# Second unit's queries and values fetched behind six weight items, and the first unit's last scores ahead of dummy products

## The chip, the cores and the metric

The kernel runs on one core of a Trainium2 chip. The metric is the device time of one execution in microseconds (us), the median of several runs. Before the change it is 558.18 us (three runs: 558.14, 558.18 and 559.48).

A core has five instruction queues, each in order: PE (matrix products; PEld are its weight loads), DVE (vector engine), ACT (scalar engine, with lookup functions), POOL (a second, slower vector engine) and SP (issues most transfers). ACT issues a few transfers too. The transfers of SP's queue and of ACT's queue are carried by the same 16 DMA engines.

## The reference

An attention-like recurrence over 768 tokens for 4 batches of 8 heads of width 48, followed by a two-layer network of width 2048 with an ELU. Cut to what matters:

```python
f = 1.0 / (1.0 + np.exp(-f_logit))
for t in range(S):
    state = f[:, :, t, :, None] * state + np.einsum('bhd,bhe->bhde', k[:, :, t], v[:, :, t])
    y[:, :, t] = np.einsum('bhd,bhde->bhe', q[:, :, t], state)
x = y.transpose(0, 2, 1, 3).reshape(B * S, H * D)          # 3072 tokens x 384
h = x @ w_in                                               # 384 -> 2048
g = np.where(h > 0.0, h, np.exp(np.minimum(h, 0.0)) - 1.0)
out = g @ w_out                                            # 2048 -> 384
```

The weights reach the chip as 8-byte floats and are turned into 4-byte floats there.

## The kernel before

The 3072 tokens are cut into 12 **units** of 256 tokens. A unit's attention is computed in a chunked form (four chunks of 64 tokens), its result `xt` is 384 x 256, and the network then runs over it in eight pieces of 256 of the 2048 inner columns. All of it is one list per engine, written out by hand in program order (`manual_schedule`); a dictionary `plan` attaches attention work of unit u+1 and weight work to numbered steps T of the network, two steps to a piece: `up(P)` at even T (h = x @ w_in for a piece), `down(P - 2)` at odd T. From unit 1 on the products use seven instead of eight blocks (`up7`), for which POOL prepares differences of blocks of `xt` (`blend`, line 892) and of weights (`mix`, line 885).

**Attention of a unit.** The 8 heads lie as four pairs; the fourth pair (number `NKT` = 3) has its gates spread over gap rows of the other three and gets them by a transfer from SBUF to SBUF (`move`, line 643, two transfers each). `gates` (lines 617 and 619) makes 1 + exp(-f) on ACT; `grow` (631) is a running product on DVE; `fall` (636) its reciprocal; `scale` (626) multiplies k by the one and q by the other on POOL. `transposed` (674) turns k by products with the identity, `advance` (737) makes the state updates of the chunks, `scores` (714) the products of k and q, `mask` (722) zeroes the later tokens on DVE, `step` (695, 700) carries the state from chunk to chunk. For unit 0 `first_outputs` (817) makes the result from scores, values and states, and ACT and DVE copy it to `xt0` (827, 829), after which the network starts (`up(0)`, line 949). For unit 1 `both(1)` at step 8 runs `advance`, `scores`, `mask` and `step`; its transposes are at step 2, its `move(1, 1)` is issued by ACT at step 3, `carried(1)` ends its result at step 11 and sends the fourth pair's rows to the gap rows of `xt1` by two transfers from ACT (line 784). `blend(1)` waits for these, and `up(8)`, the first piece of unit 1 (line 904), for `blend(1)`.

**Weights.** There are 16 items of 768 KB, in the order in which they are needed: w_in pieces 0, 1, 2, then w_out 0, w_in 3, w_out 1, w_in 4 (items 0 to 6), w_out 2 (item 7), w_in 5 (item 8), w_out 3 (item 9), w_in 6, w_out 4, w_in 7, w_out 5, 6, 7 (items 10 to 15). `fetch(n)` issues one from SP: a w_out item is one transfer (line 549), a w_in item is one large (551) and two small ones for the gap rows (554). There are seven landing buffers (`area`, `AHEAD` = 7), so `fetch(n + 7)` stands behind `merge(n)`. An item is converted by `split` (568 and 572, DVE), `lower` (578, ACT) and `merge` (586, DVE). The first two items (`HOLD` = 2) are fetched at once; items 2 to 6 wait for a small POOL memset of their buffers (line 1142) that POOL reaches behind its work for unit 0.

**Dummy products.** `warm(n)` (line 1074) issues n products of the identity of 128 x 512 whose results nobody uses.

**What orders the transfers.** Each transfer reports to one of eight completion semaphores, handed out in turn over SP's and ACT's transfers together, and its issue waits until the transfer before it on the same semaphore has landed. SP issues in order, so one waiting issue holds all behind it.

Of the kernel before, what the change touches and what calls it, by code (L numbers as in the profile page):

```python
# [356 lines left out]
def fast(ctx: ExitStack, tc: tile.TileContext, q, k, v, f_logit, w_in, w_out, out, flag, outer):  # L357
# [18 lines left out]
    nc = tc.nc  # L376
# [10 lines left out]
    HP = H // 2  # L387
    NFT = DFF // 128
    NKT = DM // 128
# [36 lines left out]
    qkf = [  # L426
        {n: cst.tile([128, HP, 2, U] if n == "f" else [128, HP, U], FP32, name=f"{n}{i}") for n in "fqk"}
        for i in range(NB)
    ]
# [5 lines left out]
    def load(u, names="fkqv"):  # L435
        b, s0 = u // UPB, (u % UPB) * U
        for n in names.replace("v", ""):
            to = qkf[u % NB][n][MAIN]
            frm = src[n][b, :, :, s0 : s0 + U].rearrange("(p r) d s -> (r d) p s", r=2)
            if n == "f":  # L440
                to, frm = to[:, 0:NKT, 0], frm[:, 0:NKT]
            nc.sync.dma_start(out=to, in_=frm)
            for r in range(2 if n == "f" or n == "k" and u > 1 else 0):
                gap = qkf[u % NB][n][GAP[r] : GAP[r] + PAD, 0:NKT]
                nc.sync.dma_start(
                    out=gap[:, :, 0] if n == "f" else gap,
                    in_=src[n][b, 2 * NKT + r, :, s0 : s0 + U].rearrange("(i j) s -> i j s", i=PAD),
                )
        if "v" in names:
            nc.sync.dma_start(  # L450
                out=vs[u % NB][:, :, PAD : PAD + DM], in_=v[b, s0 : s0 + U].rearrange("(c t) n -> t c n", t=W)
            )
# [86 lines left out]
    def fetch(n):  # L539
        if n >= NFT:  # L540
            return
        j, out_ = parts[n]
        c = slice(j * 256, (j + 1) * 256)
        to = wo[:, 2 * j : 2 * j + 2] if out_ else wi[j][:]
        if wide:
            raws[n] = area[:, n % AHEAD]
            to = raws[n].rearrange("p (k f) -> p k f", k=to.shape[1])
        if out_:
            nc.sync.dma_start(out=to, in_=w_out[c, :].rearrange("(n p) f -> p n f", n=2))
            return  # L550
        nc.sync.dma_start(out=to[MAIN], in_=w_in[0 : NKT * 2 * D, c].rearrange("(k q) f -> q k f", k=NKT))
        rest = w_in[NKT * 2 * D :, c].rearrange("(r d k) f -> r d k f", r=2, d=PAD)
        for r in range(2):
            nc.sync.dma_start(out=to[GAP[r] : GAP[r] + PAD], in_=rest[r])
# [19 lines left out]
    def lower(n):  # L574

        if wide and n < NFT:
            raw = raws[n]
            nc.scalar.activation(raw.bitcast(U16)[:, 2::4], raw.bitcast(U32)[:, 0::2], AF.Copy, scale=2.0**-29)  # L578

    def merge(n):  # L580
        if wide and n < NFT:
            hi = raws.pop(n).bitcast(I32)[:, 1::2]
            j, out_ = parts[n]
            to = wo[:, 2 * j : 2 * j + 2] if out_ else wi[j][:]
            bits, hi = (x.rearrange("p (k f) -> p k f", k=to.shape[1]) for x in (held.pop(n)[:], hi))
            nc.vector.tensor_tensor(out=to.bitcast(I32), in0=bits, in1=hi, op=ALU.add)
        fetch(n + AHEAD)
# [24 lines left out]
    def gates(u, pieces=(NKT,), bias=1):  # L612

        p = 0
        for n in pieces:
            a = qkf[u % NB]["f"][:, p : p + n, 0]
            nc.scalar.activation(a, a, AF.Exp, scale=-1.0)
            if bias:
                nc.scalar.activation(a, a, AF.Copy, bias=1.0)
            p += n  # L620

    def scale(u, *todo):

        t = qkf[u % NB]
        for n, p, e in todo:
            e.tensor_tensor(out=t[n][:, p], in0=t[n][:, p], in1=t["f"][:, p, "kq".index(n)], op=ALU.mult)  # L626

    def grow(u, p):

        g = qkf[u % NB]["f"][:, p, 0]  # L630
        nc.vector.tensor_tensor_scan(out=g, data0=g, data1=g, initial=1.0, op0=ALU.mult, op1=ALU.max)

    def fall(u, p):

        f = qkf[u % NB]["f"]
        nc.vector.reciprocal(f[:, p, 1], f[:, p, 0])  # L636

    def move(u, which, queue):

        f = qkf[u % NB]["f"]  # L640
        for r in range(2):
            to = PAD + D * r
            queue.dma_start(out=f[to : to + D, NKT, which], in_=f[GAP[r] : GAP[r] + PAD, 0:NKT, which])
# [10 lines left out]
    def watch(u):  # L654
        nc.vector.scalar_tensor_tensor(
            out=fine[:], in0=qkf[u % NB]["f"][:, 0:NKT, 0, U - 1 :], scalar=LIMIT, in1=fine[:],
            op0=ALU.is_le, op1=ALU.mult,
        )
# [44 lines left out]
    def scores(u, banks=("a0", "a1"), pairs=range(HP), pc=None):  # L703

        t = qkf[u % NB]
        if pc is None:
            ats[u] = sb.tile([128, 2, NW, HP, C], FP32, tag="at", name=f"at{u}", bufs=1)
            pc = [ps.tile([128, NW, HP, C], FP32, tag=banks[r], name=f"psS{u}_{r}") for r in range(2)]
        for p in pairs:
            for w in range(NW):  # L710
                for b in range(2):
                    cols = slice(w * W + b * C, w * W + b * C + C)
                    for r in range(2):
                        nc.tensor.matmul(  # L714
                            pc[r][FULL[b], w, p], lhsT=t["k"][FULL[r], p, cols], rhs=t["q"][FULL[r], p, cols],
                            start=True, stop=True,
                        )
        return pc
# [8 lines left out]
    def advance(u, pairs=range(HP)):  # L727

        if u not in pus:
            pus[u] = [ps.tile([128, NW, HP, D], FP32, tag=n, name=f"psU{u}_{n}") for n in ("a0", "a1")]  # L730
        pu = pus[u]
        for p in pairs:
            for w in range(NW):
                for r in range(2):
                    h = 2 * p + r
                    for b in range(2):
                        nc.tensor.matmul(  # L737
                            pu[b][FULL[r], w, p], lhsT=kn[FULL[b], p, w, FULL[r]],
                            rhs=vs[u % NB][FULL[b], w, PAD + h * D : PAD + (h + 1) * D],
                            start=(w == 0 and p == 0), stop=(w == NW - 1 and p == HP - 1), skip_group_check=True,  # L740
                        )
# [91 lines left out]
    def at_step(step, *todo):  # L833
        plan.setdefault(step, []).extend(todo)
# [233 lines left out]
    def warm(n, bank="m0", small=0):  # L1068

        pw = ps.tile([128, 4, 128], FP32, tag=bank, name="psW")  # L1070
        for _ in range(small):
            nc.tensor.matmul(pw[0:1, 0, 0:1], lhsT=ident[:, 0:1], rhs=ident[:, 0:1], start=True, stop=True)
        for _ in range(n):
            nc.tensor.matmul(
                pw[:], lhsT=ident[:], rhs=ident[:].unsqueeze(1).broadcast_to([128, 4, 128]), start=True, stop=True
            )
# [1 line left out]

    gates(0, (1, 2))
    fetch(0)  # L1080
    load(1, "kqv")
    for n in range(1, HOLD):
        fetch(n)
    warm(W0, "m3")
# [7 lines left out]
    fall(0, 0)  # L1092
    scale(0, ("q", 0, nc.gpsimd))
    warm(WA, "m3")
    gates(1, bias=0)
    advance(0, (0, 1))
    pc = scores(0, ("m2", "m3"), (0,))
    nc.gpsimd.tensor_copy(
        even_v[:, :, :, PAD:],
        vs[0][:, :, PAD : PAD + NKT * 2 * D].rearrange("t w (p r d) -> t w p r d", r=2, d=D)[:, :, :, 0],  # L1100
    )
    fall(0, 1)
    scale(0, ("k", NKT, nc.gpsimd), ("q", 1, nc.gpsimd))
    fall(0, 2)
    move(0, 1, nc.scalar)
    warm(4)
    transposed(0, 1, "m1", (1,))
    advance(0, (2,))
    scores(0, None, (1,), pc)
    scale(0, ("q", 2, nc.gpsimd))  # L1110
    advance(0, (3,))
    scores(0, None, (2,), pc)
    nc.gpsimd.tensor_copy(
        padded_v[:, :, :, PAD : 2 * PAD].rearrange("t w (r j) k -> t w r j k", r=2),
        vs[0][:, :, PAD + NKT * 2 * D : PAD + DM].rearrange("t w (r k j) -> t w r j k", r=2, j=NKT),
    )
    a = qkf[1]["f"][:, 0:NKT, 0]
    nc.vector.tensor_scalar_add(a, a, 1.0)
    for p in range(NKT):
        grow(1, p)  # L1120
    move(1, 0, nc.sync)
    scale(0, ("q", NKT, nc.gpsimd))
    warm(2)
    scores(0, None, (NKT,), pc)
    warm(1)
    fall(1, 0)
    split(0)
    for c in range(NC - 1):
# [13 lines left out]
        nc.gpsimd.memset(area[:, HOLD:].bitcast(I32)[:, :, 0:1], 0)  # L1142
    for n in range(HOLD, AHEAD):
        fetch(n)
    merge(0)
    first_outputs(0)
    first_outputs(1)
    lower(1)
    scale(1, ("k", 0, nc.gpsimd), ("q", 0, nc.gpsimd), ("k", 1, nc.gpsimd), ("k", 2, nc.gpsimd))
    scale(1, ("k", NKT, nc.gpsimd))  # L1150
    fall(1, 2)
    watch(0)
    watch(1)
    scale(1, ("q", 1, nc.gpsimd), ("q", 2, nc.gpsimd))
    at_step(A1[2], lambda: outputs(1, ("m3", "m0")), lambda: lower(A1[2]), lambda: lower(A1[2] + 1))
    for n in range(1, NFT):
        t = min(max(needs[n][0] - 2, 0), n) + 2 * (n == NFT - 1)
# [105 lines left out]
```

## Time and profile before

| | us |
|---|---|
| runs, median (lowest, highest) | 558.18 (558.14, 559.48) |
| profiled execution: its own time | 559.46 |
| profiled execution: span of the trace | 557.7 |
| PE busy in the span | 543.0 (97%) |
| DVE / ACT / POOL busy | 406.4 / 228.3 / 287.8 |
| PE busy in 0 to 14, 14 to 28, 28 to 42, 42 to 56, 56 to 70, 70 to 84 | 10.12, 11.47, 11.96, 13.79, 13.24, 14.00 |

The profile is one execution, taken by the hardware profiler; its own time is 1.76 us more than the span of the trace, and lies at the upper of the times seen. The timeline lists instructions by start (us from the start of the span), duration, engine, source line, operation, output and inputs, with the idle time of the engine before them in brackets and what ended it. Stretches give the busy time of each engine in a window, the clock granted to PE as a share of full speed, the mean busy share of the DMA engines, and GB/s. The list of waits gives for an engine and line the total wait in us, how often, and the longest. A product of 4-byte floats stands as two matrix instructions, so `warm(2)` shows as x4.

### The profile page before, as it was taken

To read this page: it belongs to the slowest core of one execution; us is meant where nothing else is said; L and a number is where in the kernel's file an instruction comes from. 1 tells how busy PE (TensorE), PEld (TensorE's weight loads), DVE (VectorE), ACT (ScalarE), POOL (GpSimd) and SP (SyncE) were. 2 spreads that over 40 slices of the span, in tenths; PEclk is the share of its full clock that TensorE was granted. 3 is DMA by queue.
4 is the path that set the end of the run, shared out by engine and by line. 5 is a ranking of instruction groups with operands and counts; after the bars stand their busy time and mean duration, and the time that the engine had idled before them with its cause. 6 is when DMAs were issued, how large, how long until landed. Compare 5 with 4: busy or idle time off the path is not lost.

```text
span 557.7 us, 15617 instructions
## 1 busy us (share of the span) xinstructions
PE 543.0 (97%) x6358; PEld 507.9 (91%) x6358; DVE 406.4 (73%) x804; ACT 228.3 (41%) x443; POOL 287.8 (52%) x559
## 2 busy tenths in 40 slices
PE   7889999999999999999999999999999999999996
PEld 3477679999999999999999999999999999999996
DVE  8799888887676776786785785786686687745553
ACT  3279764333434343333434334343343344333331
POOL 6600786475473474375465366357258258325332
PEclk9899999999999999999999999999999999999998
DMA  8998971033035135216217207307307302301001
GB/s 211 261 264 214 278 184 43 4 84 88 3 82 146 30 76 149 63 34 186 68 22 186 81 9 192 87 8 192 86 9 191 88 9 72 88 5 33 31 2 35
DMA packets 39474, 54.30 MB, mean 97 GB/s; under 512 B 4032, under 2 KB 29216, under 8 KB 39392
## 3 DMA queue, kind: packets, MB, share of 16 engines
q1 hardware_dynamic: 38592, 52.61, 36.5%
q8 instruction: 52, 0.85, 0.6%
q10 hardware_dynamic: 800, 0.59, 0.4%
q14 instruction: 30, 0.25, 0.2%
HBM read 45.02 MB, written 4.72 MB: 89 GB/s over the span
## 4 chain that ended last, share of the span: by engine, by line
PE 91%; DMA 2%; DVE 2%; ACT 1%; POOL 1%; issue 1%; SPq 1%; ACTq 0%; DVEq 0%; POOLq 0%
PE psH L904 39%; PE psM L1015 37%; PE psM L981 3%; PE psH L949 2%; PE psY L752 2%; PE psY L772 2%; PE psU_a L737 2%; PE psS L714 2%; PE psT L674 1%; DMA area<-in_moe_w_out_dram 1%; DMA f<-f 1%; ACT area L578 1%; DVE f L636 1%; POOL q L626 1%; DMA f<-in_f_logit_dram 0%
## 5 line engine op out<-in xcount | busy, mean ns | idle before, releaser
L904 PE MATMUL psH<-xt,wi 128*128 128x128 f32 (+1 forms) x1056 | 195.0, 294 | 0.0
L968 POOL TENSOR_TENSOR sums<-gg 128x128 f32<-128x128 f32 x172 | 75.6, 460 | 207.8 <-DVE gg L958 188.1
L936 ACT ACTIVATE gg<-hh 128x512 f32<-128x512 f32 x88 | 55.5, 630 | 249.3 <-DVE hh L926 111.7
L904 PEld LDWEIGHTS psH<-xt,wi 128*128 128x128 f32 x1056 | 149.5, 192 | 1.6
L904 PE MATMUL psH<-xt,area 128*128 128x128 f32 x704 | 121.5, 275 | 0.0
L904 PEld LDWEIGHTS psH<-xt,area 128*128 128x128 f32 x704 | 106.5, 192 | 4.5
L913 DVE TENSOR_TENSOR hh<-psH,u 128x256 f32<-128x256 f32 x88 | 36.9, 419 | 97.8 <-ACT u L911 97.7
L1015 PE MATMUL psM<-area,sums 128*128 128x192 f32 x516 | 99.9, 326 | 0.0
L1015 PEld LDWEIGHTS psM<-area,sums 128*128 128x128 f32 x516 | 86.0, 190 | 0.3 <-issue 0.2
L1015 PE MATMUL psM<-wo,gg 128*128 128x192 f32 x376 | 77.7, 332 | 0.0
L958 DVE SCALAR_TENSOR_TENSOR gg<-gg,hh 128x512 f32<-128x512 f32 x88 | 63.8, 725 | 1.5 <-ACT gg L937 1.5
L636 DVE RECIPROCAL f<-f 128x256 f32<-128x256 f32 x36 | 62.7, 1747 | 1.3
L937 ACT ACTIVATE gg<-gg 128x512 f32<-128x512 f32 x96 | 60.6, 631 | 3.0
L1015 PEld LDWEIGHTS psM<-wo,gg 128*128 128x128 f32 x376 | 60.2, 190 | 1.3
L926 DVE TENSOR_TENSOR hh<-psH,u43h 128x256 f32<-128x256 f32 (+1 forms) x176 | 54.6, 352 | 3.0
L626 POOL TENSOR_TENSOR q<-q,f 128x256 f32<-128x256 f32 x48 | 39.6, 826 | 19.5 <-DMA f<-f 12.9
L968 POOL TENSOR_TENSOR sums<-gg,sums 128x128 f32<-128x128 f32 x86 | 45.4, 528 | 6.7
L626 POOL TENSOR_TENSOR k<-k,f 128x256 f32<-128x256 f32 x48 | 39.3, 821 | 10.2 <-DMA f<-f 8.3
L926 DVE TENSOR_TENSOR u43h<-psH,hh 128x256 f32<-128x256 f32 x88 | 37.0, 420 | 9.2 <-PE psH L904 8.7
L968 POOL TENSOR_TENSOR sums<-sums,gg 128x128 f32<-128x128 f32 x86 | 43.0, 500 | 0.0
L1015 PE MATMUL psM<-area,gg 128*128 128x192 f32 x172 | 42.0, 326 | 0.0
L1015 PE MATMUL psM<-wo,sums 128*128 128x192 f32 x172 | 42.0, 326 | 0.0
(102 smaller groups left out, 646.3 us busy)
## 6 DMA issues: line engine op xcount, KB each, us to landing
area<-in_moe_w_out_dram SPq DMA_DIRECT2D x8, 768.0 KB, 10.6
again<-in_moe_w_in_dram SPq DMA_DIRECT2D x16, 384.0 KB, 3.6
again<-in_moe_w_out_dram SPq DMA_DIRECT2D x16, 384.0 KB, 3.6
k<-in_k_dram SPq DMA_DIRECT2D x12, 384.0 KB, 4.5
q<-in_q_dram SPq DMA_DIRECT2D x12, 384.0 KB, 5.6
v<-in_v_dram SPq DMA_DIRECT2D x12, 384.0 KB, 5.8
area<-in_moe_w_in_dram SPq DMA_DIRECT2D x8, 576.0 KB, 8.3
out_dram<-o SPq DMA_DIRECT2D x42, 96.0 KB, 2.4
```

Source lines behind the costliest of these rows:

```text
L626: e.tensor_tensor(out=t[n][:, p], in0=t[n][:, p], in1=t["f"][:, p, "kq".index(n)], op=ALU.mult)
L636: nc.vector.reciprocal(f[:, p, 1], f[:, p, 0])
L714: nc.tensor.matmul(pc[r][FULL[b], w, p], lhsT=t["k"][FULL[r], p, cols], rhs=t["q"][FULL[r], p, cols], start=True, stop=True,)
L904: nc.tensor.matmul(to, lhsT=lhs, rhs=rhs, start=(n == 0), stop=True, skip_group_check=True)
L913: add = lambda to, x, y: nc.vector.tensor_tensor(out=to, in0=x, in1=y, op=ALU.add)
L926: add = lambda to, x, y: nc.vector.tensor_tensor(out=to, in0=x, in1=y, op=ALU.add)
L936: nc.scalar.activation(g[:], h, AF.Relu, scale=-1.0)
L937: nc.scalar.activation(g[:], g[:], AF.Exp, scale=-1.0)
L958: nc.vector.scalar_tensor_tensor(out=g[:], in0=g[:], scalar=-1.0, in1=phs.pop(P), op0=ALU.add, op1=ALU.max)
L968: nc.gpsimd.tensor_tensor(out=s[:, i], in0=x, in1=y, op=op)
L981: nc.tensor.matmul(pm[t][:], lhsT=g[:, i, t * 128 : (t + 1) * 128], rhs=wo[:, 2 * j + i, :], start=(j == 0 and i == 0), stop=(j == NP - 1 ...
L1015: nc.tensor.matmul(pm[bank][:, half * DH : (half + 1) * DH], lhsT=x, rhs=y, start=first, stop=(j == NP - 1), skip_group_check=True,)
```

## The change

Parts, all in the opening of the kernel and in the order of instructions there:

1. `load(1, "kqv")` becomes `load(1, "k")`; unit 1's q and v are issued by SP behind items 1 to 6 (`load(1, "qv")` after the loop of fetches).
2. Unit 1's gates get their + 1 on ACT (`gates(1)`) and no longer on DVE (old line 1118).
3. Unit 0's pairs 1 and 2: POOL scales their q ahead of the fourth pair's k; their scores are each preceded by `warm(1)` and no longer stand behind the fourth pair's transposes.
4. The fourth pair: `warm(4)` ahead of its transposes becomes `warm(2)`; its scores stand ahead of the following `warm(2)`, not behind it; POOL copies `padded_v` behind the fourth pair's q, not ahead of it. The `warm(1)` behind the scores moves behind `first_outputs(1)`.
5. Unit 1's scaling on POOL: all four k first, then q of pairs 0 to 2.

```diff
     fetch(0)
-    load(1, "kqv")
+    load(1, "k")
     for n in range(1, HOLD):
         fetch(n)
...
     warm(WA, "m3")
-    gates(1, bias=0)
+    gates(1)
     advance(0, (0, 1))
     pc = scores(0, ("m2", "m3"), (0,))
...
-    fall(0, 1)
-    scale(0, ("k", NKT, nc.gpsimd), ("q", 1, nc.gpsimd))
-    fall(0, 2)
+    advance(0, (2,))
+    for p in range(1, NKT):
+        fall(0, p)
+        scale(0, ("q", p, nc.gpsimd))
+        warm(1)
+        scores(0, None, (p,), pc)
     move(0, 1, nc.scalar)
-    warm(4)
+    scale(0, ("k", NKT, nc.gpsimd))
+    warm(2)
     transposed(0, 1, "m1", (1,))
-    advance(0, (2,))
-    scores(0, None, (1,), pc)
-    scale(0, ("q", 2, nc.gpsimd))
     advance(0, (3,))
-    scores(0, None, (2,), pc)
+    for p in range(NKT):
+        grow(1, p)
+    move(1, 0, nc.sync)
+    scale(0, ("q", NKT, nc.gpsimd))
+    scores(0, None, (NKT,), pc)
+    warm(2)
     nc.gpsimd.tensor_copy(
         padded_v[:, :, :, PAD : 2 * PAD].rearrange("t w (r j) k -> t w r j k", r=2),
...
-    a = qkf[1]["f"][:, 0:NKT, 0]
-    nc.vector.tensor_scalar_add(a, a, 1.0)
-    for p in range(NKT):
-        grow(1, p)
-    move(1, 0, nc.sync)
-    scale(0, ("q", NKT, nc.gpsimd))
-    warm(2)
-    scores(0, None, (NKT,), pc)
-    warm(1)
     fall(1, 0)
     split(0)
...
     for n in range(HOLD, AHEAD):
         fetch(n)
+    load(1, "qv")
     merge(0)
     first_outputs(0)
     first_outputs(1)
     lower(1)
-    scale(1, ("k", 0, nc.gpsimd), ("q", 0, nc.gpsimd), ("k", 1, nc.gpsimd), ("k", 2, nc.gpsimd))
-    scale(1, ("k", NKT, nc.gpsimd))
+    warm(1)
+    for p in range(HP):
+        scale(1, ("k", p, nc.gpsimd))
     fall(1, 2)
     watch(0)
     watch(1)
-    scale(1, ("q", 1, nc.gpsimd), ("q", 2, nc.gpsimd))
+    for p in range(NKT):
+        scale(1, ("q", p, nc.gpsimd))
```

In the built program the transfers change their completion semaphores with their order. Two waits that matter: before, SP's two small transfers of item 8 wait for items 5 and 6, and item 9 and the large transfer of item 10 wait for the two transfers of `move(1, 1)`. After, the two small transfers of item 8 wait for the two transfers of `move(1, 1)`, and item 9 stands behind them in SP's queue.

## The prediction

> **What bounds the kernel now.** I read the stretches first. From 70 us on PE is busy all the time (14.00 of 14.00 us in 70 to 84), so the end moves only if PE's work of the opening moves and nothing later takes the gain back. The timeline of the opening shows what holds PE there:
>
> ```profile
> 19.57 0.72 POOL L626 TENSOR_TENSOR q<-q,f 128x256 f32<-128x256 f32 x1
> 19.57 3.35 PE L1074 MATMUL psW<-ident 128*128 128x512 f32 x4
> 20.93 0.32 SPq L551 DMA_DIRECT2D area<-in_moe_w_in_dram  x1
> 22.85 0.46 PE L714 MATMUL psS<-q,k 64*64 64x64 f32 x16
> 23.43 1.29 DVE L722 TENSOR_TENSOR at<-psS,twice 128x512 f32<-128x512 f32 x2 [3.47 <-PE psS L714]
> 28.66 0.48 ACT L827 COPY xt<-psY 128x384 f32<-128x384 f32 x1 [1.80 <-PE psY L817]
> 30.28 2.86 PE L949 MATMUL psH<-xt,wi 128*128 128x256 f32 x12 [1.67 <-DVE xt L829]
> ```
>
> The fourth pair's q is ready at 20.29, but its scores stand behind `warm(2)` until 22.85. DVE waits 3.47 us for them; mask, `first_outputs`, the copies and the first network product (30.28) follow in a chain. So the opening loses some 2.5 us to dummies. They are slow there, 0.84 us each, as the stretches show (columns: us; busy and count of PE, PEld, DVE, ACT, POOL; PE clock; DMA share; GB/s):
>
> ```profile
> 20.00:21.00 1.00, 1.00 (x2) 0.41 (x2) 0.00 (x0) 1.00 (x1) 1.00 (x6) 0.50 1.18 277
> 21.00:22.00 1.00, 1.00 (x2) 0.34 (x1) 0.00 (x0) 0.28 (x1) 1.00 (x2) 0.50 0.88 114
> 22.00:23.00 1.00, 1.00 (x10) 0.15 (x12) 0.00 (x0) 0.00 (x0) 1.00 (x3) 0.83 0.83 173
> 23.00:43.00 20.00, 17.35 (x270) 13.44 (x266) 17.68 (x26) 12.51 (x15) 3.01 (x4) 1.00 1.05 266
> 44.00:45.00 1.00, 1.00 (x6) 0.90 (x5) 1.00 (x2) 0.97 (x3) 0.00 (x0) 1.00 0.10 35
> 45.00:46.00 1.00, 1.00 (x7) 0.87 (x6) 0.95 (x2) 1.00 (x2) 0.31 (x1) 1.00 0.00 0
> 47.00:68.00 21.00, 20.24 (x316) 15.06 (x315) 19.80 (x32) 16.52 (x18) 8.94 (x13) 1.00 1.04 292
> ```
>
> The same rows show the second limit. The DMA engines are full from 23 to 43 and from 47 to 68, and empty at 45. SP's list of waits and the timeline say why, and where this reaches PE again:
>
> ```profile
> SPq L549 <- DMA f<-f: 5.8, 1, 5.8
> ```
>
> ```profile
> 40.04 0.57 ACTq L643 DMA_DIRECT2D f<-f  x1
> 45.42 0.39 SPq L549 DMA_DIRECT2D area<-in_moe_w_out_dram  x1
> 72.10 3.07 POOL L892 TENSOR_TENSOR xt<-xt 128x128 f32<-128x128 f32 x5 [2.18 <-DMA xt<-xt]
> 75.19 0.38 PE L904 MATMUL psH<-xt,wi 128*128 128x128 f32 x2
> ```
>
> Item 9 (45.42) waits from 39.6 for a transfer of `move(1, 1)`, issued at 40.04 and landed 5.3 us later. From it on weights stream without a pause; behind them land the gap rows of `xt1` (issued at 66.45 and 67.11, 5.3 and 4.8 us to landing: 71.9), then `blend(1)`, then `up(8)`. Blend's third operation ends at 74.22 and the product that reads it loads its weight at 75.3; the fifth ends at 75.17, its reader at 76.42. So **the slack of this second chain is 1.1 us**.
>
> **The change part by part.**
>
> *Scores ahead of dummies.* The fourth pair's q still waits for `move(0, 1)` (issued at 13.93, 5.4 us to landing), so I leave its end at 20.29. Scores 20.3 to 20.75, mask (1.29) to 22.05. Now `warm(2)` stands between scores and `first_outputs`. If the clock stays halved until 22.35 as before (by the shares in the rows, 0.97 in 18 to 19 and 0.83 in 22 to 23, it was halved from 18.9 to 22.35), 1.9 of four dummies are done by then and 2.1 run at 0.46 us (the eight from 11.96 took 3.70): end 23.3. Before, the bulk of `first_outputs` began at 24.77 behind the second mask. Gain 1.5 us; 2.2 with a full clock (20.75 + 4 x 0.46 = 22.6); 0 if the clock stays halved throughout. I take 1.5: the window before the halving, 15.5 to 18.9, has idle stretches in both kernels.
>
> The Trainium skill (TensorE: Matmul & The Clock Gate, Part 1) says the clock halves after an idle window of about 3.4 us. Here it halved after 1.6 us of idling, so the row goes against it. By the page the dummies would run at full clock and the gain be 2.2.
>
> *Pairs 1 and 2 earlier, + 1 on ACT.* DVE loses 0.62 us (line 1118), ACT gains an operation like L617's 0.85 ahead of its `move(0, 1)`: ACT is free at 13.53, where the move was issued at 13.33, so 0.2 us later. The cover is POOL's 4.88 us of idling ahead of 16.48; without it the 0.2 would stand ahead of the scores. The shorter dummies (x8 to x2, x2, x4) run while PE waits for the fourth pair's k (1.60 us idle); nothing.
>
> *Unit 1's q and v.* Two transfers of 0.39 MB leave SP's queue at 13.5 and enter it behind item 6. Their readers are late: scaling on POOL, idle for 12.87 us before 45.69, and `advance(1)` at 48.82. So the move itself is free for them. But items 2 to 6 don't start earlier: they wait for POOL's memset (20.8), which keeps its place within 0.3 us (padded_v's 0.45 behind q, no longer ahead). The DMA engines then have nothing between about 19.5 and 21.9, where they were moving q and v.
>
> Count bytes from 21 us until `move(1, 1)` has landed. Before: 114 + 173 + 20 x 266 + 120 + 35 = 5.76 MB (the 120 is the row of 43). After: items 2 to 7 (0.786 MB each), the large part of item 8 (0.59), q and v (0.79), the moves (0.10): 6.19 MB. So 0.43 MB more stand ahead of it. By 266 GB/s that is 1.6 us, by 292 1.5; as q and v moved at about 275 in 14 to 20, and the stretch may run faster, I take 1.4. Bounds: -0.4 (all of it at 292: 21.2 us from 21.9, and the 1.9 us tail of before) and 2.0 (the start at 21.9 costs another 0.4, as in the ramp from 45.42 to the full row at 47).
>
> *The wait that moves.* Item 8's two small transfers now wait for `move(1, 1)`. Behind them in SP's queue stand item 9 and all after it; for these wait DVE's splits, ACT's lowers and, through the stream, the gap rows of `xt1`. Each small issue takes 0.6, so item 9 goes out 1.2 us after the landing, not 0.1: L = 1.4 + 1.2 = **2.6 us later** (0.8 to 3.2). Item 8 lands near 49.8; its split stood at 48.50, so DVE is held 1.3 us there, and at item 9 by 50.08 + 2.6 - 50.55 = 2.1. Most merges are 2 to 4 us ahead of their products (item 8's merge ended at 54.4, its product began at 58.29), which covers it; the tightest, item 13, ended at 70.75 for a product at 72.61: 1.9.
>
> *The sum.* From 47 to 68 the stream is full, so `xt1`'s rows land about 2.4 us later (0.2 less than L, as one of the next unit's small loads now issues behind them). Minus the slack of 1.1: `up(8)` starts 1.3 us later than before. The 1.5 us won at 30 us are spent in waiting there. 559.46 + 1.3 = **560.8 us**. Against the median: the runs lie at two levels, 558.16 and 559.47, and the profile at the upper. An execution that is early in the opening can gain no more than the 1.1 us of slack before, and nothing after, so I take 560.8 for both: 0.5% over the median. With L at 0.8 the rows land within the slack and PE keeps 0.5: 559.0; with 3.2: 561.6.
>
> *Unit 1's k ahead of q.* The k transposes at 32.8 find k scaled at 25.1 already; free, and 0.7 us of cover more.
>
> **Rivals.**
>
> *A, no change.* The stream makes up for the bytes (the bound of 0.8), or `move(1, 1)` gets out earlier with the opening's gain. For it: GB/s vary from 178 to 382 per us within 23 to 43. Against: the move is behind q, v, items 7 and 8 wherever it is issued. 558.2 to 559.5.
>
> *B, faster.* `move(1, 1)` doesn't queue behind SP's transfers: issued at 38.5 and 39.1, landed after 2.5 us like the kernel's first load (2.48 in the chain that ended last), and 0.6 for the last small issue: item 9 goes out near 42.3, 3 us earlier, and PE keeps the 1.5. 559.46 - 1.5 = 558.0, or 556.7 from the lower level. It decides if the landing comes before 42.7 (45.42 - 1.5 - 1.2). Against it: the six such moves that ACT issues took 4.6 to 5.4 us to landing, always behind a full stream. The skill speaks for it (DMA: Bandwidth & Descriptors, Queues, rings and completion order: an engine takes turns between queues, packet by packet); by that rule the sum would be 558.0. The rows differ, and decide.
>
> *C, worse.* DVE's lateness at item 9 (2.1) plus a late tail passes the 1.9 of item 13 and the slack too: 562.
>
> **How the numbers follow.** Forecast 0.55, A 0.22, B 0.18, C 0.05. A measurement of this kernel tells 0.3% (1.7 us) from no change, so slower begins at 559.85. The forecast's own range, 559.4 to 561.6, lies above it for nine tenths: 0.50, with C 0.55. Faster needs 556.5: two thirds of B, from the lower level and with a little more than 1.5, 0.12. The rest, 0.33, is the same. The range of 558.0 to 562.0 leaves out most of B (0.14) and the far end of C.
>
> **What would show it.** Right: fourth scores near 20.3; the first network product near 28.8; DMA near zero at 20 to 22; SP waiting at a small item-8 transfer (L554) for `f<-f` until about 46.8; item 9 issued near 48; POOL waiting at L892 until about 74.5, and PE at L904 for it. Wrong: item 9 out before 45.4, or no wait of PE ahead of its first L904.

## The result, and the profile after

| | before | after |
|---|---|---|
| median (lowest to highest), us | 559.39 (557.87 to 560.37) | 562.01 (559.49 to 565.40) |
| profiled execution, us | 559.46 | 562.31 |
| span of its trace, us | 557.7 | 560.6 |

The ratio is 1.0053, with a 95% interval of 1.0035 to 1.0072: the change costs 0.5%; the medians differ by 2.6 us. With more runs of the kernel before, its median is 559.39, not the 558.18 of the first three.

The timeline of the opening, after the change (start, duration, engine, line, operation; in brackets the idle time ahead of it and what ended it):

```profile
20.43 0.73 POOL L626 TENSOR_TENSOR q<-q,f 128x256 f32<-128x256 f32 x1 [3.02 <-DMA f<-f]
...
21.22 0.71 PE L714 MATMUL psS<-q,k 64*64 64x64 f32 x16 [2.40 <-POOL q L626]
21.86 3.78 PE L1074 MATMUL psW<-ident 128*128 128x512 f32 x4
...
22.04 0.11 POOL L1139 MEMSET area<- 128x5 int32 x1
...
22.05 1.29 DVE L722 TENSOR_TENSOR at<-psS,twice 128x512 f32<-128x512 f32 x2 [2.07 <-PE psS L714]
...
22.18 0.32 SPq L551 DMA_DIRECT2D area<-in_moe_w_in_dram  x1
...
31.20 0.55 DVE L829 COPY xt<-psY 64x384 f32<-64x384 f32 x1 [3.25 <-ACT xt L829]
...
31.81 0.48 PE L949 MATMUL psH<-xt,wi 128*128 128x256 f32 x1 [0.61 <-DVE xt L829]
```

The scores come earlier (21.22, before 22.85), and so does the mask (22.05, before 23.43). But PE stood 2.40 us ahead of them, the two dummies behind them took 3.78 us, and the first network product is 1.5 us later (31.81, before 30.28). POOL's memset stands behind the fourth pair's q; it ran at 22.04 (before 20.80), and item 2, which waits for it, went out 1.25 us later (22.18, before 20.93). The stretches say why, and what the DMA engines did meanwhile (us; busy time and count of PE, PEld, DVE, ACT, POOL; PE clock; DMA share; GB/s). After:

```profile
18.00:20.00 2.00, 0.45 (x16) 0.33 (x16) 1.14 (x3) 1.45 (x3) 0.00 (x0) 1.00 0.77 138
20.00:22.00 2.00, 0.78 (x17) 0.66 (x17) 0.00 (x0) 1.00 (x1) 1.56 (x5) 0.60 0.01 5
22.00:24.00 2.00, 2.00 (x3) 0.97 (x4) 1.92 (x4) 0.00 (x0) 2.00 (x5) 0.50 0.35 44
24.00:26.00 2.00, 2.00 (x18) 0.50 (x21) 2.00 (x2) 0.00 (x0) 1.00 (x2) 0.50 1.02 307
26.00:28.00 2.00, 1.97 (x92) 1.69 (x84) 1.92 (x4) 0.00 (x0) 0.00 (x0) 0.70 1.01 244
...
46.00:48.00 2.00, 2.00 (x10) 1.58 (x9) 1.93 (x5) 2.00 (x2) 0.00 (x0) 1.00 0.23 65
48.00:50.00 2.00, 2.00 (x12) 0.93 (x13) 1.54 (x3) 1.97 (x3) 1.39 (x1) 1.00 0.17 55
```

The same stretches of the kernel before:

```profile
20.00:22.00 2.00, 2.00 (x3) 0.75 (x3) 0.00 (x0) 1.27 (x1) 2.00 (x7) 0.50 1.03 195
22.00:24.00 2.00, 2.00 (x20) 0.62 (x18) 0.57 (x1) 0.00 (x0) 1.63 (x3) 0.91 0.96 257
...
44.00:46.00 2.00, 2.00 (x11) 1.77 (x10) 1.95 (x3) 1.97 (x4) 0.31 (x1) 1.00 0.05 17
46.00:48.00 2.00, 2.00 (x8) 1.26 (x7) 1.98 (x3) 1.96 (x2) 0.58 (x1) 1.00 0.67 180
```

Two things. By the clock's shares it is halved from 20.4 to 27.2 (0.60 in 20 to 22, 0.70 in 26 to 28), before from 18.9 to 22.35; so the dummies and the first part of `first_outputs` (it runs from 25.57 to 30.1) ran at half the clock. And the DMA engines, full in 20 to 22 before, move 5 GB/s there; a second, nearly empty stretch, at 44 to 47 before, is now at 46 to 50. The list of waits and the timeline show the second half of the way:

```profile
SPq L554 <- DMA f<-f: 7.4, 1, 7.4
...
SPq L551 <- POOL area L1139: 4.1, 1, 4.1
```

```profile
41.11 0.57 ACTq L643 DMA_DIRECT2D f<-f  x1
...
47.90 1.22 SPq L554 DMA_DIRECT2D area<-in_moe_w_in_dram  x2
...
49.22 0.53 SPq L549 DMA_DIRECT2D area<-in_moe_w_out_dram  x1
...
75.34 3.08 POOL L892 TENSOR_TENSOR xt<-xt 128x128 f32<-128x128 f32 x5 [0.28 <-DMA xt<-xt]
...
76.75 0.38 PE L904 MATMUL psH<-xt,wi 128*128 128x128 f32 x2
...
77.52 0.49 PE L904 MATMUL psH<-xt,area 128*128 128x128 f32 x2 [0.39 <-POOL xt L892]
```

Two lines of the kernel before, for comparison:

```profile
20.80 0.10 POOL L1142 MEMSET area<- 128x5 int32 x1
...
75.42 0.39 PE L904 MATMUL psH<-xt,area 128*128 128x128 f32 x2
```

`move(1,1)` is issued 1.1 later than before; item 8's small transfers wait for it until 47.90; item 9 goes out at 49.22 (before 45.42). `blend` starts at 75.34 (72.10). PE reaches line 904 at 76.75 without a wait, by itself 1.56 later than before (75.19), as late as its first network product was; inside `up(8)` it then waits 0.39 us for `blend`. The second product of line 904 is the one to watch: it stands at 75.42 before and at 77.52 after. From there to the end of the profiled execution it is 484.0 us before and 484.8 after, and in the sixteen profiles of this study between 483.9 and 484.9 (559.46 - 75.42, 562.31 - 77.52, and so on). So most of what these edits did was done by this product. The rest differs by up to 1.0 us: it is 483.9 to 484.3 in the five profiles in which the second product follows the first by 0.22 us, so without a wait for `blend` (before, e1, e2, e10, e12), and 484.2 to 484.9 in the others.

### The profile page after: what moved, and what is told of

Same layout as the page of the kernel before. It is cut to its first block, busy times and chain, and to the rows that moved or that the text cites. A ratio compares the mean times of both kernels' runs of the same rounds, so it can differ in the third digit from the quotient of the medians.

```text
span 560.6 us, 15615 instructions
## 1 busy us (share of the span) xinstructions
PE 545.2 (97%) x6358; PEld 507.9 (91%) x6358; DVE 405.4 (72%) x803; ACT 229.3 (41%) x444; POOL 290.3 (52%) x559
## 4 chain that ended last, share of the span: by engine, by line
PE 86%; DVE 5%; DMA 3%; ACT 3%; issue 2%; POOL 0%; SPq 0%; ACTq 0%; DVEq 0%; POOLq 0%
PE psH L904 39%; PE psM L1015 36%; PE psY L752 2%; PE psY L772 2%; PE psU_a L737 2%; PE psS L714 2%; ACT area L578 1%; PE psT L674 1%; PE psM L981 1%; DMA area<-in_moe_w_out_dram 1%; DVE f L636 1%; DMA xt<-xt 1%; DVE wi L586 1%; DVE bits L568 1%; DMA f<-f 1%
## 5 line engine op out<-in xcount | busy, mean ns | idle before, releaser
L904 PE MATMUL psH<-xt,wi 128*128 128x128 f32 (+1 forms) x1056 | 195.0, 294 | 0.0
L904 PEld LDWEIGHTS psH<-xt,wi 128*128 128x128 f32 x1056 | 149.5, 192 | 1.6
L904 PE MATMUL psH<-xt,area 128*128 128x128 f32 x704 | 121.7, 275 | 0.4 <-POOL xt L892 0.4
L904 PEld LDWEIGHTS psH<-xt,area 128*128 128x128 f32 x704 | 106.5, 191 | 5.2 <-POOL xt L892 0.6
L626 POOL TENSOR_TENSOR q<-q,f 128x256 f32<-128x256 f32 x48 | 40.8, 852 | 25.2 <-DMA q<-in_q_dram 17.1
```

Source lines behind the costliest of these rows:

```text
L904: nc.tensor.matmul(to, lhsT=lhs, rhs=rhs, start=(n == 0), stop=True, skip_group_check=True)
```

## The experiments

All ratios are to the kernel before on the same chip, with 95% intervals. The kernels fall by two things, where unit 1's q and v stand in SP's queue and which opening they have:

| kernel | q and v | opening | ratio | first network product, second product of L904 (profile) |
|---|---|---|---|---|
| before | ahead of item 1 | old | 1 | 30.28, 75.42 |
| changed | behind item 6 | new | 1.0053 (1.0035 to 1.0072) | 31.81, 77.52 |
| e1 | ahead of item 1 | new | 1.0015 (1.0003 to 1.0027) | 32.76, 77.00 |
| e8 | ahead of item 1 | new, dummies | 1.0023 (1.0008 to 1.0038) | 29.10, 74.31 |
| e3 | behind item 3 | new | 1.0064 (1.0040 to 1.0088) | 30.30, 77.15 |
| e4 | behind item 6 | new, dummies | 1.0060 (1.0040 to 1.0081) | 29.87, 78.94 |
| e5 | behind item 6 | old, k ahead of q | 1.0033 (1.0013 to 1.0052) | 28.01, 74.28 |
| e6 | behind item 6 | new, memset early | 1.0038 (1.0021 to 1.0056) | 31.95, 76.34 |
| e7 | behind item 6 | new, move early on ACT | 1.0076 (1.0050 to 1.0103) | 31.00, 77.23 |
| e9 | behind item 6 | new, move on POOL | 1.0061 (1.0041 to 1.0082) | 30.55, 76.99 |
| e10 | ahead of item 1 | old, move on POOL | 1.0047 (1.0028 to 1.0066) | 28.56, 75.65 |
| e11 | behind item 6 | old, k ahead of q, move on POOL | 1.0077 (1.0054 to 1.0100) | 28.15, 76.08 |
| e12 | behind item 1 | new | 1.0024 (1.0009 to 1.0038) | 30.97, 75.56 |
| e13 | behind item 1 | old, k ahead of q | 0.9999 (0.9985 to 1.0013) | 29.91, 76.11 |
| e14 | behind item 1 | new, dummies | 1.0009 (0.9991 to 1.0027) | 29.37, 75.94 |

Executions of one kernel differ by up to 6 us, so a profile shows a mechanism and the ratios decide. e5's and e8's profiled executions (558.97 and 558.71) are among the lowest of theirs (medians 561.10 and 559.80), e13's (560.67) is the highest of its twelve.

### Opening or transfers: e1 to e4

**e1_open_only.** The changed kernel, and

```diff
-    load(1, "k")
+    load(1, "kqv")
...
-    load(1, "qv")
```

> The changed kernel with unit 1's q and v fetched ahead of items 1 to 6 again, so only the opening is reordered; in the built program item 9 and item 10 wait for move(1,1) again, as before the change. Theory Q (the loss comes from q and v standing ahead of move(1,1), and from the transfers of items 8 and 9 that wait for it): no loss is left, 559.4 (558.2 to 560), item 9 goes out at 44 to 46, up(8) starts near 75.5 whatever the opening does. Rival O (the loss comes from the opening: the fourth pair's q lands later, and PE's clock is halved for two stretches of 3.4 us): 561 to 562, with the first network product near 31.8 as in the changed kernel.

560.40 us, ratio 1.0015. Between the two: most of the loss is gone with q and v back in their place, but not all. The profile has the opening in its worst form (first product at 32.76, the fourth pair's q at 22.09), and no wait of PE from 46 to 84: there PE's own lateness sets the end.

**e2_qv_only.** The kernel before, and

```diff
-    load(1, "kqv")
+    load(1, "k")
...
         fetch(n)
+    load(1, "qv")
     merge(0)
```

> The kernel before with only one edit: unit 1's q and v behind item 6. In the built program the semaphores fall so that neither item 8 nor item 9 waits for move(1,1); that move waits for item 6's small transfers. Theory Q: without the wait there is nothing to lose, item 9 goes out near 42 to 43 (before: 45.42) and the rows of xt1 land earlier than before: 558.0 to 559.4. Rival O: as before, 559.4, since the opening's order is the old one. Third possibility, bytes alone (q and v push the stream back by 1.5 us, of which 1.1 is slack): 559.8 to 560.5.

570.38 us, ratio 1.0193 (1.0164 to 1.0223). No theory had this. POOL's order explains it; the timeline of POOL, then of PE:

```profile
41.46 0.72 POOL L626 TENSOR_TENSOR q<-q,f 128x256 f32<-128x256 f32 x1 [18.99 <-DMA q<-in_q_dram]
42.14 2.09 POOL L626 TENSOR_TENSOR k<-k,f 128x256 f32<-128x256 f32 x3
```

```profile
42.91 2.06 PE L674 MATMUL psT<-ident,k 128*128 128x128 f32 x6 [11.18 <-POOL k L626]
```

In the old order q of pair 0 stands ahead of three k; POOL waits 18.99 us for it, and PE 11.18 us for the k. So part 5 of the change, "k ahead of q", isn't an extra: the move needs it.

**e3_qv_item3.** The changed kernel, q and v issued when n is 4 in the loop of fetches, so behind item 3.

```diff
     for n in range(HOLD, AHEAD):
+        if n == 4:
+            load(1, "qv")
         fetch(n)
-    load(1, "qv")
```

> The changed kernel, with q and v issued behind item 3 rather than behind item 6. The same bytes stand ahead of move(1,1) and the opening is the same; but now item 9 and the large transfer of item 10 wait for the move, not item 8's two small transfers. Theory Q: item 9 goes out 1.0 to 1.2 us earlier than the changed kernel's 49.22 (two issues of 0.6 less behind the wait), up(8) as much earlier: 560.8 to 561.2. Rival O: 562.0, nothing changed in the opening.

562.29 us, 1.0064: no gain. Item 9 did go out 1.6 us earlier (47.63) and landed earlier (52.2, changed kernel 54.3), but from item 11 on nothing is left of that (60.9, changed kernel 60.6). So it isn't seen to matter which of SP's issues waits for `move(1,1)`: the two ratios differ by 0.1%, with an uncertainty of 0.3%.

**e4_after_dummies.** The changed kernel, and

```diff
+    warm(2)
     scores(0, None, (NKT,), pc)
     warm(2)
```

> The changed kernel with warm(2) more ahead of the fourth pair's scores, where PE waited 2.40 us for its q; nothing else. If the idle time is what halved the clock, the clock is full or halved for one stretch only, and the first network product comes 1.5 to 2 us earlier (near 30). Theory Q: the gain is spent waiting at the first L904, the end moves by 0.3 at most: 561.7 to 562.0. Rival O: the end moves with the first product: 560.0 to 560.7.

562.67 us, 1.0060. The opening is mended: no halved clock there, and the first product at 29.87 rather than 31.81. The end isn't. The timelines of DVE and then of PE show what it runs into:

```profile
48.50 0.56 DVE L568 TENSOR_SCALAR bits<-area 128x768 int32<-128x768 int32 x1 [3.94 <-DMA area<-in_moe_w_out_dram]
...
55.84 0.56 DVE L568 TENSOR_SCALAR bits<-area 128x768 int32<-128x768 int32 x1 [2.65 <-DMA area<-in_moe_w_out_dram]
```

```profile
58.25 0.32 PE L752 MATMUL psY<-at,v 64*64 64x64 f32 x2 [1.57 <-DVE at L722]
```

DVE waits for items 7 and 9 to land, and PE for DVE; from 60.25 to 63.66 the clock is halved in this profile. With q and v in the full stream, the earlier first product gained nothing in this kernel.

### Is it the wait for the move? e5 to e7, e9 to e11

**e5_move_and_k_first.** e2_qv_only with POOL's new order:

```diff
-    scale(1, ("k", 0, nc.gpsimd), ("q", 0, nc.gpsimd), ("k", 1, nc.gpsimd), ("k", 2, nc.gpsimd))
-    scale(1, ("k", NKT, nc.gpsimd))
+    for p in range(HP):
+        scale(1, ("k", p, nc.gpsimd))
...
-    scale(1, ("q", 1, nc.gpsimd), ("q", 2, nc.gpsimd))
+    for p in range(NKT):
+        scale(1, ("q", p, nc.gpsimd))
```

> The kernel before with two edits of the change: q and v behind item 6, and on POOL all of unit 1's k ahead of its q (in e2_qv_only POOL waited until 41.46 for q of pair 0 with three k behind it). The opening has its old order, and item 8's small transfers wait for move(1,1) as in the changed kernel. Stream theory (q and v, no longer moved while items 2 to 6 still wait for POOL's memset, are put into the full stream ahead of move(1,1) and item 9): 561.0 to 562.0, with DMA near idle at 20 to 22. Rival, the opening: 559.4, as nothing of it is reordered.

561.10 us, 1.0033: as the stream theory said. The old opening with q and v moved has the larger part of the loss.

**e6_memset_early.** The changed kernel, POOL's memset moved up behind `scale(0, ("k", NKT, nc.gpsimd))`.

```diff
     scale(0, ("k", NKT, nc.gpsimd))
+    if wide:
+        nc.gpsimd.memset(area[:, HOLD:].bitcast(I32)[:, :, 0:1], 0)
     warm(2)
```

> The changed kernel with POOL's memset of the landing buffers ahead of the fourth pair's q, so that item 2 is issued near 18.5 and not at 22.18. Stream theory: the idle stretch of the DMA engines at 19.5 to 23 is gone, all items come 2 to 3 us earlier, item 9 at 46 to 47, and the end is that of the reordered opening alone: 560.2 to 560.6. If what counts is the wait for move(1,1) by itself (issued by ACT at 41 in any case, some 5 us to landing): 561.5 to 562. Rival, the opening: 562.0.

560.76 us, 1.0038. The direction of the stream theory, not its full size: the memset ran at 17.51, but item 2 went out only at 20.46, as its completion semaphore had last been given to the first transfer of `move(0,1)`, which landed just then. Item 9 went out at 47.81, 1.4 earlier than in the changed kernel. The lines:

```profile
17.51 0.11 POOL L1111 MEMSET area<- 128x5 int32 x1
20.46 0.32 SPq L551 DMA_DIRECT2D area<-in_moe_w_in_dram  x1
...
41.27 0.57 ACTq L643 DMA_DIRECT2D f<-f  x1
...
46.51 1.20 SPq L554 DMA_DIRECT2D area<-in_moe_w_in_dram  x2
47.81 0.53 SPq L549 DMA_DIRECT2D area<-in_moe_w_out_dram  x1
```

ACT issued `move(1,1)` no earlier than in the changed kernel (41.27 against 41.11), and yet SP's wait for it ended 1.4 us earlier (46.51 against 47.90), with item 2 out 1.7 us earlier. In this profile it is the start of the stream, not ACT's issue, that sets when the move lands. By the ratio (1.0038 against 1.0053) the gain is within the uncertainty of 0.25%.

**e7_move_early.** The changed kernel, `move(1,1)` issued by ACT behind `fall(1, 2)`.

```diff
     fall(1, 2)
+    move(1, 1, nc.scalar)
     watch(0)
...
-    at_step(F1, lambda: move(1, 1, nc.scalar))
```

> The changed kernel with move(1,1) issued by ACT right behind first_outputs and unit 1's last reciprocal (near 31), not at step 3 (41.1). The bytes of the stream are the same, the DMA engines still idle at 20 to 22; but the move lands near 36 to 40, and neither item 8 nor item 9 waits for it. If the wait is what costs: item 9 at 42 to 44, up(8) set by PE's own work, 560.2 to 560.6. If only the later stream counts: 561.2 to 562. Rival, the opening: 562.0.

562.97 us, 1.0076. The wait was not removed but handed on: the semaphores now make item 6's small transfers wait for the move, 10.0 us, until 38.9, with the DMA engines at a share of 0.02 in 38 to 40. It tells nothing of a kernel without the wait.

**e9_after_pool_move, e10_before_pool_move, e11_move_pool.** The same edit with POOL as issuer, which has completion semaphores of its own, in the changed kernel, in the kernel before, and in e5_move_and_k_first.

```diff
     fall(1, 2)
+    move(1, 1, nc.gpsimd)
     watch(0)
...
-    at_step(F1, lambda: move(1, 1, nc.scalar))
```

> The changed kernel with move(1,1) issued by POOL behind unit 1's k (near 30), and so on a queue and on completion semaphores of its own; no issue of SP waits for it (in e7_move_early the wait had only moved, to item 6's small transfers, 10.0 us). Theory (the end follows item 9's issue, and that follows the landing of move(1,1), which is late because the opening ends late and because q and v stand ahead of it): item 9 at 41 to 44, the rows of xt1 in time, and PE's own work sets the end: first network product near 31.5, then 44.2 us to the second product of line 904 and 484.3 from there, as in e1_open_only: 559.5 to 560.5. Rival (q and v in the full stream cost, whoever waits): 561.5 to 562.5.

> The kernel before with only that edit: move(1,1) issued by POOL behind unit 1's k. Theory: SP's wait of 5.8 us ahead of item 9 is gone, but before the change PE's own work and the rows of xt1 were within 1.1 us of each other, so at most that is won: 557.5 to 558.7 beside 558.7 to 559.4. Rival (stream): no difference.

> The kernel of e5_move_and_k_first (the kernel before, q and v behind item 6, unit 1's k ahead of its q) with move(1,1) issued by POOL. Theory: the first network product comes near 28.0 as in e5_move_and_k_first, nothing waits for the move, and the end is 28.0 + 44.2 + 484.3 = 556.5 (to 558.0). Rival (q and v in the full stream cost, whoever waits): 560.5 to 561.5.

561.85, 561.04 and 562.95 us; 1.0061, 1.0047 and 1.0077. My theory of that point fell: e9 went the rival's way, e11 went beyond the rival's range, and e10 was slower than either of its cases. SP's wait for the move was gone. Item 9 as the trace lists it (line 549; the last line is its time from issue to landing), in the changed kernel:

```profile
L549 SPq DMA_DIRECT2D area<-in_moe_w_out_dram x1: 530/530/530, 49.2 to 49.2; - x1
...
DMA to landing us min/median/max: 5.1/5.1/5.1
```

and in e9_after_pool_move:

```profile
L549 SPq DMA_DIRECT2D area<-in_moe_w_out_dram x1: 531/531/531, 40.9 to 40.9; - x1
...
DMA to landing us min/median/max: 13.0/13.0/13.0
```

Issued 8.3 us earlier, it landed 0.4 us earlier: 40.9 + 13.0 = 53.9, against 49.2 + 5.1 = 54.3. The stretches of 14 us beside each other, changed kernel first, then e9:

```profile
42.00:56.00 14.00, 13.81 (x173) 10.00 (x172) 10.10 (x16) 11.35 (x10) 4.40 (x4) 1.00 0.78 211
56.00:70.00 14.00, 13.97 (x172) 9.90 (x171) 13.41 (x23) 11.20 (x13) 7.05 (x10) 1.00 1.04 308
```

```profile
42.00:56.00 14.00, 13.34 (x170) 9.48 (x169) 10.89 (x15) 10.63 (x10) 4.19 (x4) 1.00 1.05 265
56.00:70.00 14.00, 12.79 (x168) 9.41 (x167) 13.41 (x22) 10.91 (x13) 7.90 (x11) 1.00 1.06 282
```

Without the wait the engines are full throughout (share 1.05), and from 42 to 70 us 14 x (265 + 282) = 7.7 MB are moved, with the wait 14 x (211 + 308) = 7.3 MB: the 0.76 MB that the wait cost up to 56 are made up by half at 70. In e9 the gap rows of `xt1` landed 1.4 us earlier than in the changed kernel (73.8 against 75.2) and the second product of line 904 came 0.5 earlier, but the ratios show no gain (1.0061 against 1.0053). So SP's wait of 7.4 us looks large in the list of waits and is worth little. Why item 9, with nothing waiting, still needs 13 us, these runs show only as far as that the engines were busy all that time.

e10 has a price of its own, of which one profile shows this much:

```profile
31.29 2.36 DVE L568 TENSOR_SCALAR bits<-area 128x768 int32<-128x768 int32 x1
...
31.80 1.42 POOL L626 TENSOR_TENSOR q<-q,f 128x256 f32<-128x256 f32 x2
...
37.39 4.51 PE L949 MATMUL psH<-xt,wi 128*128 128x256 f32 x12 [1.64 <-DVE wi L586]
```

A split on DVE took 2.36 us, not 0.55, beside POOL's issue at 30.60 and its two scalings; PE then waited 1.64 us for weights, and its clock was halved from 38.05 to 41.46, so that the product took 4.51 us and not 2.8. In e11's profile no split took longer than 0.75 us, so a slow split isn't what that kernel pays for; what makes e10 and e11 slower stays open.

### Filled time: e8, e12, e13, e14

**e8_open_dummies** is e1_open_only with e4's `warm(2)`.

> The changed kernel with q and v fetched ahead of items 1 to 6 as before, and warm(2) more ahead of the fourth pair's scores: the reordered opening with neither the later stream nor the idle PE. If the 0.9 us that the reordered opening alone cost (e1_open_only, 560.40) comes from PE idling and its halved clock: 558.9 to 559.6, first network product near 30. If it comes from the fourth pair's q landing later: 560.0 to 560.4.

559.80 us, 1.0023. The time lies between the two cases. In the profile the clock is full and the first product at 29.10, yet beside e1 (1.0015) there is no gain: the halved clock isn't shown to be the price of the reordered opening.

**e12_qv_in_gap** is the changed kernel with q and v ahead of item 2; **e13_gap_old_opening** the same in e5_move_and_k_first; **e14_gap_dummies** is e12 with e4's `warm(2)`.

```diff
+    load(1, "qv")
     for n in range(HOLD, AHEAD):
         fetch(n)
-    load(1, "qv")
```

> The changed kernel with q and v issued behind items 0 and 1 and unit 1's moves, but ahead of item 2, so that they go out near 20 while items 2 to 6 still wait for POOL's memset; the opening is the changed one, item 9 waits for move(1,1) as before the change. Theory of filled time (q and v cost 2 us only when they stand in the full stream behind item 2, and nothing where the DMA engines would idle): the price of e1_open_only and e8_open_dummies is left, ratio 1.0015 to 1.0025 to before. Rival (the place matters little, as between e3_qv_item3 and the changed kernel): 1.005 to 1.006.

> The kernel before with unit 1's k scaled ahead of its q, and q and v issued behind items 0 and 1 but ahead of item 2: the old opening, and q and v in the gap. Theory of filled time: no price, ratio 0.997 to 1.001. Rival: 1.003, as e5_move_and_k_first.

> The kernel of e12_qv_in_gap with warm(2) more ahead of the fourth pair's scores, so that PE idles less and its clock is halved less. If the price of the reordered opening is the halved clock: 0.998 to 1.0005. If not (e8_open_dummies beside e1_open_only showed no gain): as e12_qv_in_gap, within 0.001.

560.65, 559.31 and 560.17 us; 1.0024, 0.9999 and 1.0009. e12 and e13 are where the theory of filled time put them; e14 lies between its two cases. In e13 q and v go out at 18.85 and 19.48, while item 2 waits for the memset, and the stretches have no gap:

```profile
18.00:20.00 2.00, 2.00 (x41) 1.06 (x40) 0.40 (x1) 0.37 (x1) 2.00 (x3) 1.00 1.07 278
20.00:22.00 2.00, 2.00 (x44) 1.18 (x36) 0.71 (x2) 1.56 (x2) 1.63 (x7) 1.00 0.99 221
22.00:24.00 2.00, 2.00 (x22) 0.69 (x22) 0.94 (x2) 0.59 (x1) 2.00 (x4) 1.00 1.10 267
```

In e5, with the same opening, q and v behind item 6:

```profile
20.00:22.00 2.00, 1.60 (x19) 0.62 (x18) 0.84 (x2) 1.17 (x1) 2.00 (x7) 1.00 0.01 2
```

The cleanest pair is e3 and e12: the opening is the same, item 9 waits for `move(1,1)` in both, and only the place of q and v differs, behind item 3 or ahead of item 2. Their stretch of 20 to 22, e3 first:

```profile
20.00:22.00 2.00, 1.02 (x17) 0.90 (x18) 0.19 (x1) 0.64 (x1) 1.79 (x7) 0.68 0.01 2
```

```profile
20.00:22.00 2.00, 0.52 (x17) 0.46 (x18) 0.39 (x2) 1.45 (x1) 1.30 (x4) 1.00 0.97 254
```

The ratios differ by 0.40% (1.0064 against 1.0024), so this price isn't that of another issue waiting for the move. It shows in the landing of the gap rows of `xt1`, too. With the new opening they land at 71.9 to 73.3 us in the four profiles with q and v ahead of item 2 (e1, e8, e12, e14), and at 73.8 to 76.3 in the six with them behind item 3 or 6. With the old opening e5 (72.0) and e13 (73.8) have it the other way round, but e5's profile is the third fastest of its twelve executions and e13's the slowest.

So the two parts of the change have separate prices, the first of them the surer. **q and v behind item 3 or 6 rather than ahead of item 2**: 0.34% in the old opening (1.0033 against 0.9999), 0.29% in the new one (1.0053 against 1.0024), 0.37% in the new one with dummies (e4 against e8; against e14 it is 0.51%), 0.40% for e3: 1.6 to 2.9 us, mostly 2. **The reordered opening**: 0.25% with q and v in the gap (1.0024 against 0.9999), 0.20% with them behind item 6 (1.0053 against 1.0033), 0.15% with them ahead of item 1: 0.8 to 1.4 us; with the dummies it is 0.10% (e14 against e13) and 0.27% (e4 against e5), and with the move on POOL -0.16% (e9 against e11). These differences carry the uncertainty of both ratios, 0.2 to 0.3%. For q and v each of them lies beyond it, for the opening only some do. No kernel here is shown to be faster than the one before.

## Why the prediction was right or wrong

*The sign was right, the ratio by luck.* 0.5% was forecast over the median, and 0.53% measured. But the sum added 1.3 us to the profiled execution, and the median of the first three runs, 558.18, was 1.2 us below that of twelve. Like with like, the medians differ by 2.6 us and the profiles by 2.85, twice the sum. The time, 562.01, is 1.2 us over the forecast and 0.01 us beyond the range.

*The step that failed* is "Scores ahead of dummies", which left the end of the fourth pair's q at 20.29 and took a gain of 1.5 us. The opening lost 1.5 us (31.81 against 30.28). Two terms were mis-sized. The fourth pair's q was left at 20.29 because the move's issue hardly changed; it was done at 21.16, because `move(0,1)` now took up to 6.5 us to landing. And the halved clock was to end at 22.35 as before; but it was halved from 20.4 to 27.2, twice as long and later. PE stood idle for 2.40 us up to 21.22, where before dummies ran from 19.57 on; with dummies put back there it was not halved (e4). The dummies I counted at 0.84 and 0.46 us all ran at 0.95, and the first part of `first_outputs` after them at half clock. The dummies that the change moves away from this place were the cover against just that, and the prediction, which asks of each edit what it covers, did not ask it of them.

*What this did to the sum.* L was to be 2.6 us; item 9 was 3.8 late. SP's wait for the move ended 2.5 later (47.90 against 45.42), where 1.4 was forecast, and the small transfers took 1.3, where 1.2 was. The missing 1.1 is a term that the sum has at nearly nothing: POOL's memset was to keep "its place within 0.3 us", but it stands behind the late q and ran 1.24 later, and with it the stream began 1.25 later. ACT's issue of `move(1,1)` came 1.1 later too, but in e6, with that issue as late and the stream begun earlier, the move landed earlier. The rows of `xt1` came 3.2 late, less the slack of 1.1: 2.1, which is what the second product of line 904 shows. PE's own work came there 1.56 late by itself, so the rows add only 0.5 to what the opening lost. A further 0.75 lies behind this product (484.8 against 484.0), where the sum has nothing.

*The signs.* DMA near zero at 20 to 22, SP at line 554 for the move, a late item 9 and a late `blend` stand in the profile, about 1 us later than forecast. The scores near 20.3 and the first product near 28.8 don't (21.22 and 31.81). And one of the prediction's own signs of being wrong came true: PE did not wait ahead of its first product of line 904, only 0.39 us ahead of a later one.

*But the name I gave the cause was wrong.* "The wait that moves" is in the trace, and e3 and e9 show that it isn't the price: with a wait at another issue, or with none, the ratio is the same within 0.3%. Shown is that q and v cost nothing measurable where the DMA engines would idle (e13: 0.9985 to 1.0013) and some 2 us where the stream is full (e5 against e13, the changed kernel and e3 against e12). That is the other half of the same paragraph, 0.43 MB more ahead of item 9 because the engines have nothing at 19.5 to 21.9. The prediction's "free" for the move of q and v itself was therefore the wrong word: free for its readers, not for those behind it.

*Rivals.* B, that the move is served at once, is out: from ACT's queue as from POOL's it landed 4.6 to 8.8 us after its issue (e1 and e9). Only in e2, where it was issued 2.9 us before the last transfer ahead of it landed, was it 2.7 and 3.1 us. A's time was the median of no kernel with q and v behind item 3 or later. C's 562 came out, but hardly by C's mechanism: the product that reads item 13 waited 0.21 us for it.

*Open.* What makes the reordered opening some 0.2% slower. Its halved clock explains a part at most. The mean granted clock of each execution was taken, too. In e12 four executions with 0.999 took 559.03 to 559.64 us, eight with 0.991 to 0.994 took 559.62 to 562.01; of the kernel before on the same chip, 25 executions with 0.997 or more have a median of 558.73, four below it 560.38. So within a kernel a halved clock goes with 1.6 to 1.8 us more, and in the new opening it is more frequent. But e14 has 0.997 or more in all twelve executions, and its median is still 560.17; e8 in ten of twelve, and it gains nothing beside e1. Whether the added dummies have a price of their own that eats the gain wasn't tried.

## What to carry to other kernels

Before moving a transfer later in a queue, look at what the DMA engines will carry in the time that it leaves free: if the next in line waits for something else, the time is lost and the bytes come back where the queue is full. A long wait of an issuing queue is not a cost until a landing moves: compare landings, not issues. And work that looks like waste at one place may be what keeps a clock up or an order harmless (the dummies here, the k ahead of q in e2): take such pairs apart only together.

## What the runs showed of the hardware

- Issuing a 768 KB transfer 8.3 us earlier into a full stream made it land 0.4 us earlier (13.0 us from issue to landing, not 5.1).
- PE's granted clock was halved for 3.41 us or 6.83 us in the opening of some profiles and not at all in others. In the new opening it was halved in all seven profiles without the added dummies, and in none of the three with them (e4, e8, e14; in e4 it was halved later, from 60.25). In the old opening it was halved in the profiles of the kernel before and e13, and not in those of e2, e5, e10 and e11, so the same order of work can go either way.
- The instants at which the clock changes lie whole multiples of 3.41 us apart within a profile, so its time can be cut into stretches of 3.41 us. In sixteen profiles with some 2500 such stretches at full clock, a halved clock followed each of the ten in which PE idled 1.72 us or more, two of the six with 1.64 to 1.71, and none with 1.60 or less. A halved stretch was followed by another where PE idled 0.83 us or more in it, and by full clock where it idled 0.28 us or less. In the changed kernel PE idled 2.37 us in 16.98 to 20.39, and 0.83 us in the stretch behind it, which was halved twice over.
- Where the idle time falls counts: the 1.67 us of idling ahead of the first network product of the kernel before is spread over two stretches, with 1.02 and 1.11 us idle in all, and its clock stayed full; 1.64 us in one stretch of e10 (up to 37.39) was followed by a halved clock from 38.05.
